# Query projection as block products of 256 columns, second-sweep weights from DRAM, phi turned through DRAM

## The chip, the cores and the metric

The kernel runs on one core of a Trainium2 chip. The metric is the time of one execution on the device, in microseconds (us), the median of several runs. A profile is one further execution, taken by the hardware profiler. The engines are TensorE (PE; its weight loads are shown as PEld), VectorE (DVE), ScalarE (ACT), GpSimd (POOL) and SyncE (SP), which issues nearly all DMAs from one queue that works in order.

## The reference

```python
# x: 2048 x 512; 32 heads of 16
def _A_ref(x, wqkv, w_phi, wo):
    qkv = (x @ wqkv) ...                       # q, k, v per head
    pq = einsum("bhsd,hdf->bhsf", q, w_phi)    # pk likewise
    phi_q = concat([softmax(pq), softmax(-pq)], -1)     # phi_k likewise
    kv = einsum("bhsf,bhsd->bhfd", phi_k, v)
    z  = einsum("bhsf->bhf", phi_k)
    num = einsum("bhqf,bhfd->bhqd", phi_q, kv)
    den = einsum("bhqf,bhf->bhq", phi_q, z)[..., None] + 1e-6
    return (num / den) ... @ wo
def _B_ref(x, w1, b1, w2, b2):                 # 512 -> 1792 -> 512
    h = einsum("bsd,df->bsf", x, w1) + b1
    r = where(h > 0, h, 0)
    return einsum("bsf,fd->bsd", r * r, w2) + b2
g = sigmoid((x * gate_w).sum(-1, keepdims=True))
return g * _A_ref(x, ...) + (1 - g) * _B_ref(x, ...)
```

All data are 32-bit floats.

## The kernel before

Each operand of a large matrix product is split into a rounded high part and the rest, the low part (`split`: ACT writes the high part, DVE or POOL subtracts it). `mm3` makes one product by three matmuls: high by high, high by low, low by high.

The rows are cut into 4 blocks of 512, each with 4 row chunks of 128; two chunks of a block are a pair, so there are 8 pairs. The 1792 hidden columns of the FFN (part B) are cut into 14 of 128. The kernel walks over all blocks twice. Each sweep does half of the FFN, 7 hidden column blocks `fc`, for each row block: 56 steps `t` in all, 28 in each sweep. A step has an `up` (12 matmuls into PSUM pool `ps_u`), ACT's relu, square and rounding, the low part `hl`, and two steps later four `down` (12 matmuls, which gather in four banks over the 7 steps of a block). At the end of a block, DVE adds the gathered rows to a row in SBUF: the first sweep writes it to `part` in DRAM, the second reads it back and writes the output.

Beside the FFN, the first sweep computes k and v of a pair by seven block products of 512 columns (`p1` to `p7`, with sums of the operands: `rows_make` and `rows_ready` for x, `sums_make` and `operand_ready` for the weights), phi of k (`features`), and the sums over rows `kvps` (`do_kv`). `w_phi` is folded into the weights of q and k on the chip (`fold`). The second sweep computes, pair by pair: q by `project` (12 matmuls of 512 columns a chunk); the two exponentials (`exps`: maximum, minimum, two subtractions on DVE, the exponential on ACT); their sums (`sums`); the weighting with z on POOL and the denominator (`q_phi`); and phi turned so that heads lie along partitions (`transposed`: a transpose of 32 x 32 squares on DVE, then four copies on ACT and twelve DMAs a chunk into the tile `phiT`). Then come the numerators (`numer`, 32 small matmuls a pair) and the product with `wo` (`attended`, called by `finish`, 12 matmuls a chunk), which is added to the same row as the FFN's result.

What is done beside step `t` is put in slots: slot `2t` runs before the step's `up`, slot `2t + 1` after it; the second sweep begins at slot 56. `at(slot, f, ...)` fills them. Within this, the order on each engine comes from the framework's scheduler: it goes by the order of the program, `tc.high_priority` moves an instruction ahead, and `tc.issue_after(i)` keeps an instruction behind `i` on the same engine. All waits between engines follow from the tiles.

In the first sweep the weights of a step are fetched again for each block (raw, and rounded again on ACT; the low part from `lkept` in DRAM). In the second sweep all 7 pairs of weight blocks stay in SBUF: three in the pool `fpool`, four in places of operands that the first sweep no longer needs (`ffn_tiles`).

Of the kernel before, what the change touches and what calls it, by code (L numbers as in the profile page):

```python
# [16 lines left out]
P = 128  # L17
# [13 lines left out]
AHEAD = 150  # L31
FOLD_AT = 9, 3
KEPT_LATE = ("w1", 0), ("w1", 1), ("w2", 0)
SUMS = ("t1", "t2", "t15", "k2")
# [3 lines left out]
def tile_gated_mix(ctx: ExitStack, tc: tile.TileContext, xT, xn, wqT, wkT, wphi, wv, wo, w1, b1, w2, b2, gw, out):  # L38
# [16 lines left out]
    taken = [0]  # L55

    def bank(name):
        p = banks[taken[0] % len(banks)]
        taken[0] += 1
        return p.tile([P, 512], F32, tag="s", name=name)  # L60

# [14 lines left out]

    ALL = slice(0, 512)
# [11 lines left out]
    def slots(op, kk, name, dtype=F32R):  # L91
        return [wpool.tile([P, 512], dtype, tag=f"{op}{kk}{j}", name=f"{name}{j}") for j in "hl"]

    def ffn_tiles(nm, fc):
        if fc >= NFH + NSTR:
            return slots(("B21", "T1", "T4", "T3")[fc - NFH - NSTR], int(nm == "w2"), f"{nm}{fc}")
        return (fpool.tile([P, 512], F32R, tag=nm + "h", name=f"{nm}h{fc}"),
                fpool.tile([P, 512], F32R, tag=nm + "l", name=f"{nm}l{fc}"))
# [20 lines left out]

    def again_ready(nm, fc):  # L120
# [15 lines left out]
    def x_tiles(b, k):  # L136
        return (xpool.tile([P, SB], F32R, tag="xh", name=f"xh{b}_{k}"),
                xpool.tile([P, SB], F32R, tag="xl", name=f"xl{b}_{k}"))


    def x_save(b):
        for k in range(NK):
            for j in range(2):
                nc.sync.dma_start(xkept[b, k, j], st["x", b][k][j].bitcast(F32))

    def load_x(b):
        xs = []
        for k in range(NK):
            xs.append(x_tiles(b, k))
            for j in range(2):  # L150
                nc.sync.dma_start(xs[k][j].bitcast(F32), xkept[b, k, j])
        return xs
# [31 lines left out]
    xkept = dram.tile([NB, NK, 2, P, SB], F32, name="xkept")  # L184
    lkept = dram.tile([NFH, 2, P, 512], F32, name="lkept")
    kvs = const.tile([P, 2 * P], F32, name="kvs")
# [53 lines left out]
    def foldq_fetch():  # L240
        st["wq"] = [row() for _ in range(NK)]
        for k in range(NK):
            nc.sync.dma_start(st["wq"][k], wqm[k])

    def foldq_ready(k):
        hi, lo = slots(("B11", "T2")[k // 2], k % 2, f"wq{k}")
        with tc.high_priority(offset=AHEAD):
            split(st["wq"][k], hi, lo, nc.scalar, nc.vector)
        st.setdefault("wa", []).append((hi, lo))
# [9 lines left out]
    def operand_ready(op, kk):  # L259
# [5 lines left out]
        st["W", op, kk] = hi, lo  # L265


    def rows_make(p):
        b, q = divmod(p, 2)
        a, c = (t.rearrange("p (k c s) -> p k c s", k=2, c=NC) for t in st["xr", b])  # L270
        part_of = lambda t, h: t[:, :, 2 * q + h, :]
        r = st["S", p] = [row(), row()]
        o = [r[i // 2][:, i % 2 * 2 * P:(i % 2 + 1) * 2 * P].rearrange("p (k s) -> p k s", k=2) for i in range(4)]
        for i, x, y, op in ((0, part_of(a, 1), part_of(c, 1), ALU.add), (1, o[0], part_of(a, 0), ALU.subtract),
                            (2, part_of(a, 0), part_of(a, 1), ALU.subtract), (3, part_of(c, 0), o[1], ALU.subtract)):
            nc.gpsimd.tensor_tensor(o[i], x, y, op)  # L276

    def rows_ready(p):
        if p % 2 == 0:
            his, los = ([work.tile([P, 512], F32R, tag=g, name=f"S{p}{g}{j}", bufs=2) for j in range(2)] for g in ("oh", "ol"))  # L280
        else:
            t = work.tile([P, 2, 4, NG, 32], F32R, tag="phiT", name=f"S{p}", bufs=1).rearrange("p u r g s -> p (u r g s)")
            t = [t[:, i * 512:(i + 1) * 512] for i in range(4)]
            his, los = t[:2], t[2:]
        for src, hi, lo in zip(st.pop(("S", p)), his, los):
            with tc.issue_after(st["act"].ins):
                split(src, hi, lo, nc.scalar, nc.vector)
        for i in range(4):
            for kk in range(2):
                s = slice((i % 2 * 2 + kk) * P, (i % 2 * 2 + kk + 1) * P)  # L290
                st["A", p, f"S{i + 1}", kk] = his[i // 2][:, s], los[i // 2][:, s]

# [7 lines left out]
    def load_w(src):  # L300
        res = []
        for k in range(NK):
            t = stage.tile([P, 512], F32, tag="in", name="in")
            for q in range(4):
                s = 64 * (4 * (k % 2) + q) + 32 * (k // 2)
                nc.sync.dma_start(t[32 * q:32 * q + 32, :], src[s:s + 32, :])
            if k < 2:
                hi, lo = slots("B22", k, f"wo{k}")
            else:
                hi, lo = (wpool.tile([P, 512], F32R, tag=tag, name=f"wo{tag}") for tag in SUMS[2 * k - 4:2 * k - 2])  # L310
            split(t, hi, lo, nc.scalar, nc.vector)
            res.append((hi, lo))
        return res
# [24 lines left out]
    def project(c, xs, ws, nm):  # L338
        ps = bank(nm)
        sc = slice(c * P, (c + 1) * P)  # L340
        for k in range(NK):
            mm3(ps, xs[k], ws[k], sc, ALL, k == 0, k == NK - 1)
        return ps

    def exps(ps, tag="e"):
# [6 lines left out]
        with tc.high_priority(offset=AHEAD):  # L352
            nc.vector.tensor_reduce(mx, pv, AX.X, ALU.max)
            nc.vector.tensor_reduce(mn, pv, AX.X, ALU.min)
# [517 lines left out]
```

## Time and profile before

| | |
|---|---|
| time, median of 3 runs | 508.5 us (507.81 to 508.73) |
| profiled execution | 506.81 us, its span on the core 505.0 us |
| PE busy | 500.7 us (99%), 3616 matmuls |
| PE weight loads | 404.0 us (80%) |
| DVE busy | 405.2 us (80%) |
| ACT busy | 253.9 us (50%) |
| POOL busy | 75.6 us (15%) |
| DMA | 84.79 MB, mean 168 GB/s |

Busy times are those of one engine; the engines work beside one another, so they do not add up. Matmuls follow each other before the earlier one has left the array, so the length of a row of PE is not its price; the distance between starts is. In a group's row stand the line, the engine, the operation, what it writes and reads, how often, and then the busy time in us, the mean in ns, and the idle time of the engine just before, with what ended it. In a row of the order of time stand the start and the length in us. A row of a stretch has its length and the busy time of each engine, with the number of instructions, then the granted clock of TensorE, the share of the DMA engines and GB/s.

### The profile page before, as it was taken

What the parts mean: (1) busy time and instruction counts of PE and PEld (TensorE: products, weight loads), DVE (VectorE), ACT (ScalarE), POOL (GpSimd) and SP (SyncE); (2) the same over time, 40 slices, a digit from 0 to 9 for tenths busy, and PEclk for the clock granted to TensorE, in tenths of its full rate; (3) what the DMA queues carried; (4) which work ended last, traced back from release to release, by engine and by line L of the source; (5) the groups of instructions that cost most, each with busy time, mean ns of one, the idle gap of its engine ahead of it and who ended that gap; (6) DMA issues with size and microseconds to landing.
All of it is one profiled execution on the core that took longest, in us unless ns stands there. A gap on an engine that the chain in (4) does not pass through costs nothing.

```text
span 505.0 us, 9519 instructions
## 1 busy us (share of the span) xinstructions
PE 500.7 (99%) x3616; PEld 404.0 (80%) x3616; DVE 405.2 (80%) x642; ACT 253.9 (50%) x433; POOL 75.6 (15%) x77
## 2 busy tenths in 40 slices
PE   9999999999999999999999999999999999999997
PEld 4878887788888888888888878787887878788876
DVE  4979996898877868797889898968789677798724
ACT  6598573364743646373765653443425353433530
POOL 5304020302050000000004122202122222202100
PEclk9999999999999999999999999999999999999999
DMA  8998888965657656845669161212153321032102
GB/s 296 331 361 299 232 283 270 321 234 192 212 183 245 236 165 208 279 140 155 187 183 311 51 195 52 91 51 92 39 185 96 86 74 44 8 100 82 43 22 83
DMA packets 52437, 84.79 MB, mean 168 GB/s; under 512 B 8104, under 2 KB 14504, under 8 KB 52392
## 3 DMA queue, kind: packets, MB, share of 16 engines
q1 hardware_dynamic: 52072, 83.79, 51.5%
q8 instruction: 28, 0.46, 0.4%
q10 hardware_dynamic: 288, 0.39, 0.3%
q14 instruction: 17, 0.14, 0.1%
q0 software_dynamic: 32, 0.01, 0.0%
HBM read 56.37 MB, written 21.50 MB: 154 GB/s over the span
## 4 chain that ended last, share of the span: by engine, by line
PE 97%; ACT 1%; DMA 1%; DVE 0%; issue 0%
PE d L75 10%; PE u L75 10%; PE d L77 10%; PE d L76 10%; PE u L76 10%; PE u L77 10%; PE q L75 3%; PE q L77 3%; PE att L77 3%; PE q L76 3%; PE att L76 3%; PE att L75 3%; PE ky L75 2%; PE ky L76 2%; PE ky L77 2%; PE kvps L378 2%
## 5 line engine op out<-in xcount | busy, mean ns | idle before, releaser
L459 ACT ACTIVATE r<-u,b1c 128x512 f32<-128x512 f32 x56 | 38.4, 685 | 146.1 <-PE u L77 146.0
L387 POOL TENSOR_TENSOR ez<-e,z 128x512 f32<-128x512 f32 x32 | 41.3, 1312 | 279.8 <-ACT e L358 160.5
L75 PE MATMUL d<-w2h,hh 128*128 128x512 f32 x160 | 62.7, 392 | 0.0
L77 PE MATMUL d<-w2h,hl 128*128 128x512 f32 x160 | 62.3, 389 | 0.0
L76 PE MATMUL d<-w2l,hh 128*128 128x512 f32 x160 | 62.3, 389 | 0.0
L75 PE MATMUL u<-xh,w1h 128*128 128x512 f32 x152 | 59.6, 392 | 0.1
L76 PE MATMUL u<-xl,w1h 128*128 128x512 f32 x152 | 59.2, 389 | 0.0
L77 PE MATMUL u<-xh,w1l 128*128 128x512 f32 x152 | 59.2, 389 | 0.0
L363 DVE TENSOR_REDUCE sm<-e 128x64 f32<-128x1024 f32 x32 | 38.9, 1215 | 18.5 <-ACT e L358 18.5
L464 DVE TENSOR_TENSOR hl<-r,hh 128x512 fp32r<-128x512 f32 x56 | 38.5, 687 | 13.8 <-ACT hh L463 13.7
L411 ACT ACTIVATE phiT<-tb 32x256 f32<-32x256 f32 x64 | 26.5, 413 | 32.1 <-DVE tb L405 31.4
L358 ACT ACTIVATE e<-e 128x1024 f32<-128x1024 f32 x32 | 33.8, 1056 | 11.9 <-DVE e L356 11.6
L463 ACT ACTIVATE hh<-r 128x512 fp32r<-128x512 f32 x56 | 35.3, 630 | 1.5
L460 ACT ACTIVATE r<-r 128x512 f32<-128x512 f32 x56 | 35.2, 629 | 1.3
L75 PEld LDWEIGHTS d<-w2h,hh 128*128 128x128 f32 x160 | 30.0, 188 | 6.7 <-issue 0.6
L77 PEld LDWEIGHTS d<-w2h,hl 128*128 128x128 f32 x160 | 30.0, 188 | 6.3
L76 PEld LDWEIGHTS d<-w2l,hh 128*128 128x128 f32 x160 | 30.1, 188 | 6.1
L75 PEld LDWEIGHTS u<-xh,w1h 128*128 128x128 f32 x152 | 28.5, 188 | 7.6 <-issue 0.8
L276 POOL TENSOR_TENSOR row<-xin 128x256 f32<-128x256 f32 x16 | 17.5, 1103 | 112.8 <-DVE S2ol L70 24.8
L77 PEld LDWEIGHTS u<-xh,w1l 128*128 128x128 f32 x152 | 28.5, 188 | 6.1
L76 PEld LDWEIGHTS u<-xl,w1h 128*128 128x128 f32 x152 | 28.5, 188 | 5.8
L389 DVE TENSOR_REDUCE dz<-ez 128x64 f32<-128x1024 f32 x16 | 19.4, 1210 | 9.4 <-POOL ez L387 9.3
(544 smaller groups left out, 1161.6 us busy)
## 6 DMA issues: line engine op xcount, KB each, us to landing
in<-in_w SPq DMA_DIRECT2D x66, 256.0 KB, 3.3
phiT<-tb SPq DMA_DIRECT2D x192, 32.0 KB, 1.9
w2l<-lkept SPq DMA_DIRECT2D x20, 256.0 KB, 3.7
w1l<-lkept SPq DMA_DIRECT2D x19, 256.0 KB, 4.4
xin<-in_xT SPq DMA_DIRECT2D x16, 256.0 KB, 5.0
xkept<-xh SPq DMA_DIRECT2D x16, 256.0 KB, 3.6
xkept<-xl SPq DMA_DIRECT2D x16, 256.0 KB, 4.0
in<-in_xn SPq DMA_DIRECT2D x16, 256.0 KB, 2.8
```

The lines of the kernel that those rows point to most:

```text
L75: nc.tensor.matmul(o, ah[:, sa], bh[:, sb], start=first, stop=False, **kw)
L76: nc.tensor.matmul(o, ah[:, sa], bl[:, sb], start=False, stop=False, **kw)
L77: return nc.tensor.matmul(o, al[:, sa], bh[:, sb], start=False, stop=last, **kw)
L358: nc.scalar.activation(ef, ef, AF.Exp)
L363: nc.vector.tensor_reduce(sm, e3, AX.X, ALU.add)
L387: nc.gpsimd.tensor_tensor(ez[:, hs, :], e3[:, hs, :], zbc[half], ALU.mult)
L389: nc.vector.tensor_reduce(dz, ez, AX.X, ALU.add)
L411: nc.scalar.activation(dst, src, AF.Copy)
L459: nc.scalar.activation(r, ps, AF.Relu, bias=b1c[:, fc:fc + 1])
L460: nc.scalar.activation(r, r, AF.Square)
L463: st["act"] = nc.scalar.activation(hh, r, AF.Copy)
L464: low = lambda: st.update(low=nc.vector.tensor_tensor(hl, r, hh.bitcast(F32), ALU.subtract))
```

## The change

1. q of a pair comes from seven block products of 256 columns (`q1` to `q7`), with sums of x chunks (fetched again, `rows_fetch`, and summed on POOL, `rows_again`) and of the folded weights (`foldq_sums`, on POOL). `project` goes. Results are put together by two ACT copies and five DVE additions into two rows in SBUF, from which `exps` reads.
2. The second sweep's FFN weights no longer stay. High and low part lie in one tile and are kept in DRAM (`fkept`), and each step rereads 512 KB for w1 and for w2 (`again_both`). Eleven of the fourteen are split in the first sweep (`early`, `early_ready`, `early_keep`, slots 28 to 45), low parts on POOL.
3. phi goes after DVE's transpose to DRAM in one DMA a chunk (`phi_keep`) and returns turned by four DMAs a pair (`phi_load`). The four ACT copies and twelve DMAs a chunk go.
4. From the end of the first sweep on, the order on PE, DVE and POOL is that of the program (`in_turn`, `Turns`); slots have fractions that order the work within one, and work with a fraction over 0.6 of an odd slot runs between the second and third `down`. `q_phi` is cut into `do_z`, `do_d`, `do_m`, `do_t` with slots of their own.
5. Low parts of the hidden rows `hl` go from DVE to POOL for all second-sweep column blocks but the last two, at the end of the step. Low parts of `wo` go to POOL too. `att` and `kvt` use `ps_u`.
6. High and low parts of x lie in one tile too, with one DMA for both.

```diff
-    def project(c, xs, ws, nm):
-        ps = bank(nm)
-        for k in range(NK):
-            mm3(ps, xs[k], ws[k], sc, ALL, k == 0, k == NK - 1)
...
+EARLY = tuple((nm, NFH + i) for i in range(6) for nm in ("w1", "w2"))[:11]
+HW = D // 2
...
+        def __getattr__(self, name):
+            def issue(*a, **kw):
+                with tc.issue_after(st[self.key].ins) if self.key in st else nullcontext():
+                    i = getattr(self.engine, name)(*a, **kw)
+                if "pe" in st:
+                    st[self.key] = i
+                return i
...
+    vec, pol = Turns(nc.vector, "dve"), Turns(nc.gpsimd, "pool")
...
+    def again_both(nm, fc):
+        w = up_w if nm == "w1" else down_w
+        w[fc] = ffn_tiles(nm, fc)
+        nc.sync.dma_start(st["ffn", nm, fc].bitcast(F32), fkept[fc - NFH, int(nm == "w2")])
...
-            for r in range(4):
-                dst = pt[32 * j:32 * j + 32, u, r, :, :].rearrange("p g s -> p (g s)")
-                src = tb[32 * r:32 * r + 32, 256 * j:256 * j + 256]
-                if j == r:
-                    nc.scalar.activation(dst, src, AF.Copy)
-                else:
-                    nc.sync.dma_start(dst, src)
+    def phi_keep(n):
...
+        nc.sync.dma_start(st["pk", n // 2][n % 2], st.pop(("tb", n)))
+
+    def phi_load(pair):
+        pt = st["pt", pair] = work.tile([P, 2, 4, NG, 32], F32, tag="phiT", name="phiT", bufs=1)
         for j in range(4):
+            nc.sync.dma_start(pt[32 * j:32 * j + 32].rearrange("p u r g s -> p (u r) (g s)"),
+                              st["pk", pair].rearrange("u (r p) (j c) -> j p (u r) c", p=32, c=2 * P)[j])
...
-        low = lambda: st.update(low=nc.vector.tensor_tensor(hl, r, hh.bitcast(F32), ALU.subtract))
+        eng = pol if NFH <= fc < NF - 2 else vec
+        low = lambda: st.update(low=eng.tensor_tensor(hl, r, hh.bitcast(F32), ALU.subtract))
...
+    def q1(p):
+        st["X", p] = ps_a.tile([P, 512], F32, tag="s", name="qx")[:, :HW]
+        product(st["X", p], p, "A11", "B11", True, False)
+        t = kept("t1")
+        st["t1", p], st["t2", p] = t[:, :HW], t[:, HW:]
+        with tc.high_priority(offset=AHEAD):
+            nc.scalar.activation(st["t1", p], st["X", p], AF.Copy)
+
+    def q6(p):
+        st["Y", p] = ps_b.tile([P, 512], F32, tag="s", name="qy")[:, :HW]
+        product(st["Y", p], p, "S2", "T2", True, False)
+        total(st["t2", p], st["Y", p], st["t1", p])
+
+    def q2(p):
+        product(st["X", p], p, "A12", "B21", False, True)
+        st["row", p] = [wpool.tile([P, 512], F32, tag=f"B221{j}", name=f"q{j}") for j in "hl"]
+        with tc.high_priority(offset=AHEAD):
+            nc.scalar.activation(st["row", p][0][:, :HW], st["X", p], AF.Copy)
+
+    def q5(p):
+        st["Z", p] = ps_a.tile([P, 512], F32, tag="s", name="qz")[:, :HW]
+        product(st["Z", p], p, "S1", "T1", True, False)
+        st["t15", p] = kept("t2")[:, :HW]
+        total(st["t15", p], st["Z", p], st["t1", p])
+    # q7: Y += S3 T3, row[1] right = Y + t15;  q3: Z += S4 B22, row[0] right = Z + t2
+    # q4: Y += A22 T4, row[1] left = Y + t1
...
+        for nm, s in (("w1", 2 * t - 8), ("w2", 2 * t - 4)):
+            if (nm, fc) in EARLY and t < (NB + 1) * NFH:
+                i = EARLY.index((nm, fc))
+                k = (28, 29, 30, 37, 38, 39, 40, 41, 42, 43, 44)[i]
...
+            if t < (NB + 1) * NFH and (nm, fc) not in EARLY:
+                at(s, fetch, nm, fc)
+                at(s + 2, ready, nm, fc, pol)
+                at(s + 5, keep_both, nm, fc)
+            else:
+                at(s + 1, again_both, nm, fc)
...
     for p in range(NB * NC // 2):
-            at(s + 2 * c, do_q, NB + q, n + c, n % NC + c)
-            at(s + 2 * c + 2 * (p == 0), do_q_scaled, n + c, n % NC + c)
-        at(t - 2, do_n, p)
+        m, n, s = NPAIR + p, 2 * p, 54 + 6 * p
+        at(s - 6, rows_fetch, m)
+        at(s - 5 + 3 * (p == 0), rows_again, m)
+        at(s - 2, rows_ready, m, pol)
+        for f, d in ((q1, 0), (q6, 1.2), (q2, 1.2), (q5, 2.2), (q7, 2.2), (q3, 3), (q4, 3)):
+            at(s + d + (d == 0 and p > 1) + 0.7 * (p == 1 and d == 3), f, m)
+        u = s + 3
...
+                        (do_e, 0, 0), (do_z, 0, 1), (do_e, 1, 1), (do_s, 0, 1), (do_z, 1, 2), (do_s, 1, 2.8), (do_d, 0, 2.8), (do_m, 0, 3),
+                        (do_t, 0, 3), (do_d, 1, 3), (phi_keep, 0, 4), (do_m, 1, 4.5), (do_t, 1, 4.5), (phi_keep, 1, 5.5)):
...
+        at(u + 6 - 0.5 * late, phi_load, p)
...
+        at(s + 11.7, do_n, p)
+        at(s + 13.1, finish, n, n % NC)
+        at(s + 14.1, finish, n + 1, n % NC + 1)
```

More of the change, by code (lines that the diff above doesn't have):

```diff
@@ new lines, in do_d, with do_m, do_t @@
+        vec.reciprocal(den, den)
+        w = st["w", n] = small.tile([P, H, 2], F32, tag="w", name="w", bufs=2)
+        vec.tensor_tensor(w, r.rearrange("p (h t) -> p h t", t=2),
+                          den.unsqueeze(2).to_broadcast([P, H, 2]), ALU.mult)
+    def do_m(n):
+        st["phi", n] = scaled(st.pop(("q", n))[0], st.pop(("w", n)).rearrange("p h t -> p (h t)"), vec)
+    def do_t(n):
+        tb = st["tb", n] = work.tile([P, 2 * D], F32, tag="tb", name="tb", bufs=2)
+        vec.transpose(tb, st.pop(("phi", n)))
@@ L419, in numer @@
     def numer(pt):
-        pss = [bank(f"num{r}") for r in range(2)]
+        pss = [banks[r].tile([P, 512], F32, tag="s", name=f"num{r}") for r in range(2)]
         def mm(t, q, r):
@@ L481, in up @@
         else:
[L482 to L483 removed]
+            with in_turn():
+                for k in range(NK):
+                    up_step(ps, k, xs, wf)
+            if "pe" in st:
+                st["pe"] = st["up"]
         return hidden(fc, ps, later)
```

355 lines of the change are left out of this document (205 added, 150 removed).

## The prediction

> **What bounds the kernel now.** I read the page first (busy shares, then the chain that ended last), then busy time by stretch, then the groups with their shapes kept apart, the order of time around two places, and the DMA issues.
>
> ```profile
> span 505.0 us, 9519 instructions
> ...
> PE 97%; ACT 1%; DMA 1%; DVE 0%; issue 0%
> ...
> core 0: us, PE busy (x) PEld busy (x) DVE busy (x) ACT busy (x) POOL busy (x), PEclk, DMA share, GB/s
> 0.00:250.50 250.50, 249.31 (x2172) 200.50 (x2176) 205.84 (x332) 143.66 (x240) 34.31 (x45) 1.00 0.74 242
> 250.50:502.00 251.50, 251.35 (x1449) 203.50 (x1448) 198.97 (x311) 110.25 (x193) 41.30 (x32) 1.00 0.31 94
> 280.00:480.00 200.00, 200.00 (x1069) 161.37 (x1068) 163.08 (x250) 88.24 (x157) 36.20 (x28) 1.00 0.27 81
> ...
> 125.00:205.00 80.00, 80.00 (x833) 65.87 (x833) 63.70 (x105) 44.81 (x73) 6.58 (x8) 1.00 0.64 211
> ```
>
> The chain is TensorE's own queue, 97%. In the second sweep (250.5 to 502) TensorE is idle for 0.15 us in 251.5, at a granted clock of 1.00. So there is no wait to take away: that stretch gets shorter only if TensorE gets less to do, and every new wait of TensorE adds its full length. DVE is the second load, 163.08 of 200 us (82%), with POOL at 18% and DMA at 0.27.
>
> **The sum on TensorE.** The kernel projects queries, for each of 16 row chunks, by 12 matmuls of 512 columns (four blocks of the contraction, three products each for the high and low parts): 192. The change makes them pair by pair: seven products, each 2 blocks by 3, so 42 matmuls of 256 columns for a pair, 336 for eight.
>
> ```profile
> 316.10 0.39 PE L75 MATMUL q<-wq0h,xh 128*128 128x512 f32 x1
> ...
> 318.82 0.39 PE L75 MATMUL u<-xh,w1h 128*128 128x512 f32 x1
> ...
> 500.26 0.28 PE L75 MATMUL end<-w212h,hh 128*128 128x256 f32 x1
> ...
> 500.38 0.19 PEld L77 LDWEIGHTS end<-w212h,hl 128*128 128x128 f32 x1
> ...
> 501.57 0.28 PE L77 MATMUL end<-w213h,hl 128*128 128x256 f32 x1
> ```
>
> A duration here contains the pipeline, so the price is the distance of starts. The twelve matmuls of one chunk take 318.82 - 316.10 = 2.72 us, 0.2267 each. The nearest row for the new shape is the last accumulation of the kernel, with new weights for every matmul as in the products: twelve of 256 columns start from 500.26 to 501.57, 1.31 / 11 = 0.119 each. That is a little over half; each pays some 12 ns whatever its width. Removed: 192 x 0.2267 = 43.5 us. Added: 336 x 0.119 = 40.0 us. The gain is 3.5 us, not the eighth (5.4 us) that the count of columns gives. The other matmuls keep their shapes and numbers; the numerators and the attention output move in the order only.
>
> The weight load shows 0.19 us, more than 0.119, yet the loads of these twelve keep the pace: they overlap one another and the matmuls. [...]
>
> **What the other engines gain and lose.** All of it lies beside TensorE; the cover is the time of one pair:
>
> ```profile
> 324.42 1.02 PE num L424 x32
> 352.86 1.02 PE num L424 x32
> ...
> L363 DVE TENSOR_REDUCE sm<-e 128x64 f32<-128x1024 f32 x32 | 38.9, 1215 | 18.5 <-ACT e L358 18.5
> L464 DVE TENSOR_TENSOR hl<-r,hh 128x512 fp32r<-128x512 f32 x56 | 38.5, 687 | 13.8 <-ACT hh L463 13.7
> L405 DVE STREAM_TRANSPOSE tb<-e 128x1024 f32<-128x1024 f32 x16 | 19.9, 1241 | 0.3
> L369 DVE TENSOR_TENSOR e<-e,w 128x1024 f32<-128x1024 f32 x16 | 19.6, 1223 | 0.4
> L389 DVE TENSOR_REDUCE dz<-ez 128x64 f32<-128x1024 f32 x16 | 19.4, 1210 | 9.4 <-POOL ez L387 9.3
> L365 DVE RECIPROCAL r<-sm 128x64 f32<-128x64 f32 x32 | 17.3, 541 | 0.0
> L353 DVE TENSOR_REDUCE mx<-q 128x32 f32<-128x512 f32 x16 | 10.8, 674 | 6.8 <-PE q L77 6.8
> L620 DVE TENSOR_TENSOR kvs<-kvs,kvps 128x256 f32<-128x256 f32 x8 | 3.2, 405 | 0.0
> L387 POOL TENSOR_TENSOR ez<-e,z 128x512 f32<-128x512 f32 x32 | 41.3, 1312 | 279.8 <-ACT e L358 160.5 <-DMA z<-zrow 116.9 <-DVE dz L389 2.4
> L276 POOL TENSOR_TENSOR row<-xin 128x256 f32<-128x256 f32 x16 | 17.5, 1103 | 112.8 <-DVE S2ol L70 24.8 <-DVE T10l L70 24.2 <-DMA xin<-in_xT 22.3
> L411 ACT ACTIVATE phiT<-tb 32x256 f32<-32x256 f32 x64 | 26.5, 413 | 32.1 <-DVE tb L405 31.4
> ```
>
> A pair takes 352.86 - 324.42 = 28.4 us (three up/down steps, two projections, two attention outputs, one set of numerators), 28.0 after. DVE per pair is now 0.82 x 28.4 = 23.2 us. It loses three low parts of the hidden rows (3 x 0.69), which go to POOL, and gains five additions of 256 columns (5 x 0.41, the nearest row is kvs): 23.2 again, 83%. Its low parts of second-sweep weights go to POOL, 11 of 14 in the first sweep. ACT loses the 64 copies into phiT (26.5 us) and gains two copies of 256 columns and two high parts per pair: never near its limit. POOL grows most, per pair: 4 x 1.31 for the z products as now, 3 x 1.31 hidden rows, 2 x 1.31 low parts, 4 x 1.10 row sums = 16.2 us, 58%. A hidden row's low part has more than one whole step before it is read, so I cost these at nothing.
>
> POOL's growth is not quite free for DVE:
>
> ```profile
> 265.23 2.56 POOL L387 TENSOR_TENSOR ez<-e,z 128x512 f32<-128x512 f32 x2 [116.85 <-DMA z<-zrow]
> ...
> 266.75 1.58 DVE L70 TENSOR_TENSOR w111l<-in,w111h 128x512 fp32r<-128x512 f32 x1
> 268.26 0.68 DVE L70 TENSOR_TENSOR w2l<-in,w2h 128x512 fp32r<-128x512 f32 x1
> ...
> 260.00:280.00 20.00, 20.00 (x89) 16.55 (x89) 20.00 (x31) 10.87 (x19) 5.10 (x4) 1.00 0.86 278
> ...
> L394 DVE SCALAR_TENSOR_TENSOR den<-dz,eps x16: 238/252/836, 272.0 to 473.1; 128x32 f32<-128x32 f32 x16
> ```
>
> The same subtraction takes 1.58 us beside POOL's ez and 0.68 just after it ends; den's median is 0.25 and its longest 0.84. [...] From the rows: about twelve such DVE operations a pair (four of them new, since the exponents' subtractions now read q from SBUF and not from PSUM), each meeting POOL with probability 0.58 and waiting half of a 1.31 operation on average, 0.38 x 12 = 4.6 us; some 1.4 of that is there today at 18%. Added 3 us: DVE at about 26 of 28 us. It still fits, with little to spare.
>
> **The new chain from q to the numerators.** phi was turned by 12 small DMAs and four ACT copies a chunk. Now it goes to DRAM in one DMA a chunk, and comes back by four.
>
> ```profile
> phiT<-tb SPq DMA_DIRECT2D x192, 32.0 KB, 1.9
> w2l<-lkept SPq DMA_DIRECT2D x20, 256.0 KB, 3.7
> w1l<-lkept SPq DMA_DIRECT2D x19, 256.0 KB, 4.4
> xin<-in_xT SPq DMA_DIRECT2D x16, 256.0 KB, 5.0
> part<-row SPq DMA_DIRECT2D x16, 256.0 KB, 3.3
> ...
> L67 ACT ACTIVATE xh<-xin 128x512 fp32r<-128x512 f32 x16 | 9.4, 621 | 3.4 <-DMA xin<-in_xT 3.2
> ...
> SPq L413 <- DVE tb L405: 22.6, 9, 7.8
> ```
>
> A keep of 512 KB is not in the trace: between 3.3 (part<-row, half the bytes) and 7, I take 5. The load of 1 MB in four: between 3.7 and 8, I take 6. On DVE, both chunks of a pair: four row operations (2.7), sum and reciprocal (1.75), dz and its four small ones (2.3), scaling and transpose (2.5) = 9.2 each, 18.5 for two, plus the earlier pair's low parts and additions, 3: 21.5, and 32.5 us with the DMAs. TensorE between the last product and these numerators, by the slots of the diff: four ups and four and a half downs (23.1), 42 products (5.0), two attention outputs (5.4), one set of numerators (1.3) = 35 us. Margin 2.5 us; the 3 us of contention or a block's end (four additions of 0.7) use it up. So I charge 0.5 us in all: a fraction of a microsecond at some of the eight pairs, between 0 and 1 us at every one.
>
> SP's queue is in order: a keep waits there for DVE's transpose, as the phiT issues do now (22.6 us in nine waits), and behind it stand the rereads of 512 KB weights. These have three slots and more (some 13 us) before use against a landing of 5; hidden. Rereads (53 x 0.5 MB), phi (16 MB both ways) and x rows (4 MB), less phiT and the raw weights, add some 40 MB in 251 us: 94 + 160 = 254 GB/s, about the 242 that the first sweep moves without a stall. There, eleven early weights add 8 MB in about 80 us: 211 + 103 = 314 GB/s from 125 to 205 us, at a share that 0.64 would put at 0.95; the cover is the two steps between a fetch and its use. I cost it at nothing; the other end is one late landing with its wait, 5 us. ACT, 44.81 of 80 us busy there, takes 11 more high parts of 0.62 us (xh), POOL 11 low parts and earlier row sums, at 6.58 of 80. The rest is small and has that cover too: seven query operands are split for four before, their four sums go to POOL, wo's low parts go from DVE to POOL, and pairs of 256 KB tiles become one of 512 KB with half the issues on SP.
>
> The tail (last accumulation, addition, output) and the start keep their work. Sum: 505.0 - 3.5 + 0.5 = 502.0 us of span. The profiled execution took 506.8 in all, the median of the runs is 508.5; the same 3.0 less gives **505.5 us**.
>
> **Rivals.**
> 1. phi comes late: the numerators of every pair wait about 1 us for its return, because DVE is held up by POOL. 8 x 1.0 - 3.5 = +4.5: 513 us. It decides from 0.44 us a pair. For it: DVE at 26 of 28 us and the margin of 2.5. Against: each wait gives DVE time to catch up, and DVE was at 100% from 260 to 280 with TensorE never waiting. 16%.
> 2. Nothing to measure: waits of 2.5 to 4.5 us at the products (TensorE waits for ACT's copy between the first and third product, or for an addition before it writes on the same bank) use up the gain. 508.5 us. 12%.
> 3. The loads bound the products, at 0.19 us each: 336 x 0.19 - 43.5 = +20 us, 528. The twelve rows of 0.119 speak against it. 3%.
> 4. The first sweep's DMA at 0.95 brings weights late, once or twice by a landing of 5.0 us (xin): 508.5 - 3.0 + 5.0, 510.5 us, or 515.5 for two. 7%.
>
> **How the numbers follow.** The forecast has 62%, alone 504.4 (the full gain and the scatter of runs) to 507.4. A measurement of this kernel tells about 0.2% (1.0 us) from no change. Faster: 62%; same: 12%; slower 16 + 3 + 7 = 26%. The range that leaves out two in ten reaches into rivals 1 and 4: 504.4 to 511.
>
> **What would show it.** Products 0.119 us apart; TensorE's idle time from 250 to the end still under 1 us; numerators 28.0 us apart. Wrong, if weight loads stand 0.19 apart, if the numerators wait for a DMA, if products wait for DVE or ACT, or if DVE's subtractions read 1 us and more beside POOL.

## The result: 6.7% slower

The changed kernel took 542.39 us (median of 6 runs, 538.81 to 548.4), the kernel before on the same chips 507.6 us (6 runs, 506.89 to 508.73): a ratio of 1.0665 [1.0617, 1.0714], where the brackets hold the 95% interval. The longest run, 548.4 us, was in a slower state of the chip, and the ratio leaves it out. The forecast was 505.5 us, range 504.4 to 511. The profiled execution took 539.66 us.

The page of the changed kernel (head, busy shares, and the chain that ended last):

```profile
span 537.9 us, 9771 instructions
...
PE 511.3 (95%) x3760; PEld 413.7 (77%) x3760; DVE 440.2 (82%) x647; ACT 244.7 (45%) x404; POOL 187.5 (35%) x167
...
PE 52%; DVE 23%; DMA 14%; ACT 4%; issue 3%; SPq 2%; POOL 1%; ACTq 0%; DVEq 0%; POOLq 0%
```

The chain was TensorE's own queue for 97%; now it is for 52%, and DVE and DMAs hold 37%. Busy time by stretch, with the columns of the prediction's table:

```profile
0.00:250.50 250.50, 249.00 (x2166) 200.20 (x2167) 205.33 (x326) 147.54 (x246) 59.09 (x65) 1.00 0.81 275
250.50:534.50 284.00, 262.30 (x1596) 213.47 (x1594) 234.38 (x321) 97.14 (x158) 128.42 (x103) 0.98 0.71 229
280.00:480.00 200.00, 183.83 (x1054) 149.58 (x1052) 175.99 (x235) 67.02 (x109) 99.22 (x79) 0.97 0.73 235
```

The first sweep lost nothing to speak of (249.00 us of TensorE, 249.31 before). The second is 284.0 us long instead of 251.5. TensorE is idle for 21.7 us of it, against 0.15, and its mean granted clock is 0.98. No engine is full: DVE 88%, POOL 50%. What TensorE waited for (us in total, times, longest):

```profile
PE num L474 <- DMA phiT<-phi: 11.7, 8, 2.5
PE qy L82 <- DVE t L64: 4.0, 5, 1.3
PE qz L82 <- DVE t L64: 3.4, 2, 3.2
PE qx L82 <- ACT t L683: 1.4, 1, 1.4
```

The numerators wait for phi's return from DRAM, and the products for DVE's additions, which must read a PSUM bank before a product writes it again. The order of time around the longest product wait, on PE, DVE and POOL (start, length; DVE's last line is a quiet `den` from a later pair):

```profile
291.69 0.39 PE L84 MATMUL d<-w,hl 128*128 128x512 f32 x1
295.30 0.58 PE L82 MATMUL qz<-wqB22h,S 128*128 128x256 f32 x1 [3.22 <-DVE t L64]
...
296.32 0.41 PE L83 MATMUL qz<-wqB22l,S 128*128 128x256 f32 x1
296.53 0.41 PE L84 MATMUL qz<-wqB22h,S 128*128 128x256 f32 x1
...
288.10 1.36 DVE L64 SCALAR_TENSOR_TENSOR dz<-dz,inv,r 128x64 f32<-128x64 f32 x1
289.49 1.18 DVE L64 SCALAR_TENSOR_TENSOR den<-dz,eps 128x32 f32<-128x32 f32 x1
...
291.35 2.31 DVE L64 TENSOR_TENSOR e<-e,w 128x1024 f32<-128x1024 f32 x1
293.69 1.25 DVE L64 STREAM_TRANSPOSE tb<-e 128x1024 f32<-128x1024 f32 x1
294.86 0.39 DVE L64 TENSOR_TENSOR t<-qz,t 128x256 f32<-128x256 f32 x1
...
387.52 0.25 DVE L64 SCALAR_TENSOR_TENSOR den<-dz,eps 128x32 f32<-128x32 f32 x1
...
288.08 1.29 POOL L64 TENSOR_TENSOR hl<-r,hh 128x512 fp32r<-128x512 f32 x1
289.33 1.29 POOL L64 TENSOR_TENSOR w<-in,w 128x512 fp32r<-128x512 f32 x1
291.30 1.28 POOL L64 TENSOR_TENSOR w<-in,w 128x512 fp32r<-128x512 f32 x1 [0.68 <-ACT w L74]
```

This one place holds most of the case. Read DVE against POOL: `dz` ends at 289.46, just after POOL's `hl` (289.37); `den` ends at 290.67, just after POOL's `w` (290.62), 1.18 us for work of 0.25; `e<-e,w` takes 2.31 instead of the 1.22 of before. The addition `t` that TensorE needs stands behind this phi work in DVE's written order, and the product starts 3.6 us after the matmul ahead of it (295.30 against 291.69), where 0.23 us is the pace. Then read the products: 0.21 us apart, not 0.12. The granted clock in two slices of 1 us shows why:

```profile
296.00:297.00 1.00, 1.00 (x7) 1.00 (x7) 0.01 (x1) 0.00 (x0) 0.00 (x0) 0.50 1.01 410
299.00:300.00 1.00, 1.00 (x6) 0.82 (x5) 1.00 (x3) 0.23 (x1) 0.00 (x0) 1.00 0.94 299
```

TensorE ran at half clock from 294.9 to 298.3. Four such stretches of 3.4 us (from 294.9, 308.6, 342.7 and 496.3) come at waits in this sweep or just behind them. There the loss is more than the wait: TensorE was busy for 12.9 us of the four stretches, and half of that, about 6.5 us, is my estimate of the price of the clock.

The other wait, in the chain that ended last:

```profile
390.81 1.26 DVE tb L64
...
392.09 2.91 DMA phi<-tb
...
396.37 8.07 DMA phiT<-phi
...
404.57 1.09 PE num L474 x30
```

From the end of the pair's last transpose to its numerators there are 12.5 us: the keep 2.9, 1.4 in SP's queue, the loads 8.1. (Two of the 32 matmuls of the numerators had started at 402.08; the other 30 waited.)

The account, from the distance of each matmul's start to the one before it, less the pace of its shape: numerators about 15.5 us late in all, `qy` 4.8, `qz` 3.9, `qx` 1.5, `kvps` about 2, together 27.7; half clock 6.5; less 3.3 from the products. That is about 31 of the sweep's 32.5; the rest is many small ones.

### The profile page after: what moved, and what is told of

The parts are those of the page before. It is cut to its first block, busy times and chain, and to the rows that moved or that the text cites. A ratio compares the mean times of both kernels' runs of the same rounds, so it can differ in the third digit from the quotient of the medians.

```text
span 537.9 us, 9771 instructions
## 1 busy us (share of the span) xinstructions
PE 511.3 (95%) x3760; PEld 413.7 (77%) x3760; DVE 440.2 (82%) x647; ACT 244.7 (45%) x404; POOL 187.5 (35%) x167
## 4 chain that ended last, share of the span: by engine, by line
PE 52%; DVE 23%; DMA 14%; ACT 4%; issue 3%; SPq 2%; POOL 1%; ACTq 0%; DVEq 0%; POOLq 0%
DMA phiT<-phi 8%; DVE e L64 6%; PE d L82 5%; PE d L84 5%; PE d L83 5%; PE u L82 5%; PE u L84 5%; PE u L83 5%; DMA phi<-tb 3%; DVE dz L64 3%; DVE tb L64 2%; DVE den L64 2%; PE ky L82 2%; PE ky L83 2%; PE ky L84 2%
## 5 line engine op out<-in xcount | busy, mean ns | idle before, releaser
L82 PE MATMUL d<-w,hh 128*128 128x512 f32 x222 | 89.4, 402 | 0.0
L83 PE MATMUL d<-w,hh 128*128 128x512 f32 x222 | 87.8, 396 | 0.0
L84 PE MATMUL d<-w,hl 128*128 128x512 f32 x222 | 87.5, 394 | 0.0
L82 PE MATMUL u<-x,w 128*128 128x512 f32 x216 | 84.9, 393 | 0.7 <-issue 0.6
L83 PE MATMUL u<-x,w 128*128 128x512 f32 x216 | 84.4, 391 | 0.0
L84 PE MATMUL u<-x,w 128*128 128x512 f32 x216 | 84.1, 390 | 0.0
L64 POOL TENSOR_TENSOR ez<-e,z 128x512 f32<-128x512 f32 x32 | 46.7, 1477 | 74.3 <-ACT e L405 36.6
L82 PEld LDWEIGHTS d<-w,hh 128*128 128x128 f32 x222 | 42.5, 192 | 12.4 <-issue 3.9
L84 PEld LDWEIGHTS d<-w,hl 128*128 128x128 f32 x222 | 42.4, 191 | 9.2
L83 PEld LDWEIGHTS d<-w,hh 128*128 128x128 f32 x222 | 42.6, 192 | 7.8
L82 PEld LDWEIGHTS u<-x,w 128*128 128x128 f32 x216 | 40.9, 189 | 9.8 <-issue 1.0
L84 PEld LDWEIGHTS u<-x,w 128*128 128x128 f32 x216 | 40.7, 188 | 8.7
L83 PEld LDWEIGHTS u<-x,w 128*128 128x128 f32 x216 | 40.9, 189 | 8.2
L64 POOL TENSOR_TENSOR hl<-r,hh 128x512 fp32r<-128x512 f32 x20 | 26.8, 1339 | 46.7 <-ACT hh L515 46.7
L77 POOL TENSOR_TENSOR early<-early 128x512 fp32r<-128x512 f32 x11 | 14.6, 1324 | 67.4 <-ACT early L74 54.6
L64 DVE TENSOR_TENSOR hl<-r,hh 128x512 fp32r<-128x512 f32 x36 | 29.4, 817 | 7.9 <-ACT hh L515 7.8
```

The costliest lines, as they stand in the source:

```text
L64: i = getattr(self.engine, name)(*a, **kw)
L77: st["low"] = elo.tensor_tensor(lo, src, hi.bitcast(F32), ALU.subtract)
L82: nc.tensor.matmul(o, ah[:, sa], bh[:, sb], start=first, stop=False, **kw)
L83: nc.tensor.matmul(o, ah[:, sa], bl[:, sb], start=False, stop=False, **kw)
L84: return nc.tensor.matmul(o, al[:, sa], bh[:, sb], start=False, stop=last, **kw)
```

## The experiments

Two causes stood against each other: phi's return trip through DRAM, and POOL's new reads of SBUF, beside which DVE's operations last longer (`den` 1.18 us for 0.25 above). The expectations call the first theory A, the second theory B or the port; "port" is a name here, and no run shows where in the chip DVE is held. A third was the written order on DVE. The first runs take one of them away each; the later ones take two away, measure POOL's reads by themselves, look for a remedy, and put the parts into the schedule of before. Ratios are to the kernel before on the same chip, medians in us. Where DVE's "stretch" is given, it is summed over its instructions after 250 us: what each exceeds the lower quartile of its own shape. Before it is 2.2 us, changed 37.1; these sums move by about 1 us with the way shapes are told apart.

**Part 3 undone: phi turned by ACT copies and small DMAs again.**

```diff
 def phi_keep(n):
+    for j in range(4):
+        for r in range(4):       # j == r: ACT copy; else:
+            nc.sync.dma_start(dst, part_of)
-    nc.sync.dma_start(st["pk", n // 2][n % 2], ...)
```

> The changed kernel with part 3 undone: phi goes to phiT by four ACT copies and twelve 32 KB DMAs a chunk again, at the same slots as the keeps. Theory A (the numerators wait because phi's way through DRAM, a 2.9 us keep and some 9 us of loads, is too long for the schedule): the numerators' waits (15.5 us of late starts in the changed kernel) and the half-clock stretches behind them go, span 515 to 520 us of 537.9. [...]

548.13, 1.0785 [1.0744, 1.0826]: no gain at all. TensorE's waits:

```profile
PE num L479 <- DMA phiT<-tb: 6.9, 5, 2.9
PE u L82 <- DMA w<-fkept: 6.4, 4, 3.4
```

In the kernel before, the 24 small DMAs of two chunks held SP's queue for 15.1 us (299.88 to 314.98), some 7.5 a chunk. Here the rereads of weights stand behind them and land late (`u` waits 6.4 us for them): a second wait, in place of part of the first. In the kernel before the weights stayed in SBUF, and no reread stood behind.

**phi loaded from the pair before**, so that the load need not wait for its own keep.

```diff
-  st["pk", pair]
+  st["pk", max(pair - 1, 0)]
```

> The changed kernel, but the loads of phiT read the tile that the pair before has kept (its results are of the wrong pair), so that numerators wait for no keep of their own pair; the loads, their bytes and their slots stay. Theory A: the numerators' late starts fall from 15.5 us to under 3, the products' stay near 10 us, span 517 to 522. Theory B: TensorE, no longer slowed at the numerators, outruns DVE and waits as much more at the products (for additions on the same bank): span 528 to 536.

539.72, 1.0623 [1.0582, 1.0664], no gain, but the experiment missed its aim: the load was still issued on SP behind its own pair's keep, which waits there for the transpose. TensorE's waits at the numerators fell from 11.7 to 7.3 us, and those at `qy` rose from 4.0 to 7.1. The run says nothing against the return trip as a cause.

**POOL's new work left out**: the low parts `hl`, and the sums of x for all pairs but the first. The fetches of x for these sums and ACT's high parts of them fall away too.

```diff
+  if NFH <= fc < NF - 2: return hh, hh
-  at(s - 6, rows_fetch, m); at(..., rows_again, m); at(s - 2, rows_ready, m, pol)
+  if p == 0: ...   # the same three
```

> The changed kernel with POOL's new work left out: the hidden rows' low parts of the second sweep but the last two blocks (the high part stands in their place in the products) and the sums of x and their splits for pairs 1 to 7 (pair 0's are used again, their DMAs go too). POOL falls from 16 to 5 us a pair. Theory B (the port): DVE's scaling falls back from 1.66 to 1.22 us, den from 0.82 to 0.25, the exponents' subtractions from up to 1.5 to 0.68; some 4 us a pair on DVE; late starts fall from 28 us to under 8, span 508 to 514. Theory A: DVE gets faster but phi's trip still makes the numerators late by more than 1 us a pair: span 522 to 530.

529.06, 1.0428 [1.037, 1.0485].

```profile
PE num L474 <- DMA phiT<-phi: 9.5, 6, 2.1
PE num L474 <- DVE e L64: 2.2, 1, 2.2
...
PE qy L82 <- DVE t L64: 0.6, 1, 0.6
```

The product waits are all but gone, the numerators' stay. DVE's stretch falls from 37.1 to 19.4 us.

**The written order on DVE and POOL given up** (left to the scheduler).

```diff
-  vec, pol = Turns(nc.vector, "dve"), Turns(nc.gpsimd, "pool")
+  vec, pol = nc.vector, nc.gpsimd
```

> The changed kernel without the written-out order on DVE and POOL (TensorE's order stays): the scheduler orders them again. Theory C (DVE's queue waits at its head, 20.6 us for ACT's high parts of the numerators among them, while later work is ready): waits at the products and the numerators shrink, span 520 to 528. Theories A and B: the order is not what is late, span within 5 us of 537.9, or longer.

575.1, 1.1333 [1.1296, 1.1371]. The wait moves to `qx`, whose bank is freed only by the numerators' low parts:

```profile
PE qx L82 <- DVE oo L77: 33.0, 6, 10.4
```

So the written order is better than the scheduler's. Whether a third order would be better still, this run does not tell.

**No return trip**: loads read rows kept long before, issued ahead of the keeps.

```diff
-  st["pk", pair]  ...  at(u + 6 - 0.5 * late, phi_load, p)
+  xkept[0, 0:2]   ...  at(u + 3, phi_load, p)
```

> The changed kernel with phi's return made independent of phi: the four loads of a pair read a block of the kept x (so the numerators are of x and not of phi) and stand six slots after the products start, ahead of the keeps in SP's queue; keeps, loads and bytes stay. Theory D (a loop: numerators of pair p, then DVE's low parts of them, which stand in its fixed order ahead of the next pair's sums, scaling and transposes, then keep, load and the next numerators: 33 us a turn against 28 us of TensorE): the loop is cut, DVE's idle time before the numerators' low parts (20.6 us) falls under 6, late starts at the numerators from 15.5 to under 2 and at the products from 10 to under 5, span 508 to 515. Theory B (DVE's own load is too much): the waits move to the products, span 525 to 533.

532.43, 1.0502 [1.0481, 1.0522].

```profile
PE qy L82 <- DVE t L64: 12.2, 7, 3.4
PE qz L82 <- DVE t L64: 2.0, 3, 1.4
```

No wait at the numerators, but the products now wait for DVE for 14.2 us where it was 7.4.

**Both taken away.**

> The kernel of y1 with POOL's new work left out as in x3 too (hidden rows' low parts of the second sweep but the last two blocks, x sums and splits of pairs 1 to 7). If late phi and the port together are all of the loss, TensorE's late starts in the second sweep fall under 4 us, no half-clock stretch is left before the end, and the gain on the products shows: span 501 to 506. If something else slows the second sweep (DMA, TensorE's written order), it stays above 510.

512.61, 1.0101 [1.0081, 1.0122]. By the ratios, POOL's work alone took 2.4% off the time and the return trip alone 1.6%, some 12 and 8 us; the two together took 5.6%, some 29 us, which is more than the sum. The waits above fit this: with one of them gone, TensorE comes to the other sooner. The stretch from 280 to 480:

```profile
280.00:480.00 200.00, 198.41 (x1192) 164.97 (x1191) 180.54 (x267) 68.98 (x110) 47.15 (x33) 1.00 0.79 250
```

Numerators and products in order of time:

```profile
327.36 1.09 PE L474 MATMUL num<-phiT,kvb 64*32 64x256 f32 x32
...
332.59 0.28 PE L82 MATMUL qx<-wqB11h,x 128*128 128x256 f32 x1
...
333.19 0.28 PE L84 MATMUL qx<-wqB11h,x 128*128 128x256 f32 x1
...
355.49 1.09 PE L474 MATMUL num<-phiT,kvb 64*32 64x256 f32 x32
```

First to sixth matmul of a product: 0.60 / 5 = 0.120 us. These two sets of numerators stand 28.13 us apart, forecast 28.0. So the products do what they were to do, and the clock is back at 1.00.

**The numerators' low parts later on DVE**, behind the next pair's `sm` and `dz`, as a test of the idea that DVE's waits in its order feed the loop.

```diff
-  split(pss[r], oh, ol, nc.scalar, vec)
+  nc.scalar.activation(oh, pss[r], AF.Copy)
+  at(s + 11.9, do_nl)      # the low parts
```

> The changed kernel with one edit: DVE's low parts of the numerators stand in its order behind the next pair's sums and denominators (second chunk's sums, first chunk's denominators), not ahead of them. Theory D: DVE no longer waits for the numerators with 4.6 us of work ready, the loop gets some 3 to 4 us shorter, span 518 to 528. Theory A (a long trip alone): the chain from products to numerators is no shorter, span 535 to 541.

553.01, 1.0912 [1.0887, 1.0937]. The idea fell: the low parts also free banks, and `qx` waits for them.

```profile
PE qx L82 <- DVE oo L64: 12.9, 5, 6.1
```

**phi written turned, four keeps of 128 KB, and one plain load a chunk.**

```diff
+  for j in range(4): nc.sync.dma_start(t[j].rearrange("p r c -> r p c"), tb[:, 256*j:256*(j+1)])
+  nc.sync.dma_start(st["pt", n // 2][:, n % 2]..., st["pk", n]...)   # 512 KB, contiguous
```

> The changed kernel with phi laid out in DRAM as phiT needs it: four keeps of 128 KB a chunk, then one contiguous load of 512 KB a chunk, the first chunk's a slot earlier than before. Theories A and D: the trip from the last transpose to the numerators falls from 12.4 to some 8 us, 4 us a pair: late starts at the numerators under 5 us, span 518 to 527. Theory B: DVE is late by itself, waits move to the products, span 530 to 538.

586.41, 1.1546 [1.1499, 1.1593]. From the chain of the last pair, in order of time:

```profile
487.29 7.47 DMA phi<-tb
494.83 3.88 DMA phiT<-phi
```

The waits of SP's queue:

```profile
SPq L467 <- DMA phi<-tb: 80.4, 24, 5.9
```

A load of one chunk took 3.9 us, where a pair, twice the bytes, took 8.1. The keep grew from 2.9 to 7.5 us, and a load that waits on SP for its keep holds up all that stands behind it, 80.4 us in all.

**`wo` loaded later, on top of "both taken away"**, for the wait of `kvps` (2.6 us) that was left there.

```diff
-  at(base + 10 + k, load_w, wo, k)
+  at(57 + k, load_w, wo, k)
```

> The kernel of y2 (phiT loaded from kept x, POOL's hidden-row low parts and x sums left out) with one more edit: wo is loaded and split in slots 57 to 60, not 52 to 55, so that ACT's queue does not wait for it at the turn of the sweeps. In y2 TensorE waits 2.8 us there before the last sums over rows. Theory E (what y2 still loses is the turn of the sweeps): that wait goes, span 505 to 508. If it stays, another head of ACT's or POOL's queue holds it: 509 to 512.

513.25, 1.0119 [1.0076, 1.0161]: the wait fell to 1.0 us, the time did not.

**Split sums of x kept in DRAM**, not computed again on POOL, so that the change is complete but POOL lighter.

```diff
+  at(split_at + 4, rows_save, p)     # 1 MB a pair to DRAM
-  at(s - 6, rows_fetch, m); at(..., rows_again, m); at(s - 2, rows_ready, m, pol)
+  at(s - 2, rows_load, m)
```

> The changed kernel, results whole, with the split sums of x kept in DRAM in the first sweep and read back (1 MB a pair) where the change fetches x again and forms and splits its sums on POOL. POOL loses 5.6 of 16 us a pair. Theory F (late phi and the port each hide the other): DVE's stretching falls by a quarter to a third, but the numerators still wait for the trip, so the span falls by 2 to 7 us only, 531 to 536. Theory B alone (the port is all): 520 to 527.

543.37, 1.0709 [1.0688, 1.0729]. POOL falls from 99 to 62 us in 280 to 480, but with 8 MB of keeps more, at 305 GB/s, TensorE is busy for 3.7 us less of the first sweep (249.00 in the changed kernel):

```profile
0.00:250.50 250.50, 245.35 (x2139) 196.13 (x2140) 202.04 (x322) 146.29 (x245) 55.81 (x61) 0.99 0.87 305
```

**That, `wo` late, and each chunk's loads issued on their own as early as may be.**

> The kernel of z2, results whole, with wo in slots 57 to 60, and with the first chunk's loads of phi issued ahead of the second chunk's landing, so that 512 KB and not 1 MB stand behind the last keep. Theory F: both hold-ups shrink together, the trip by some 3 us and the port by a third, which is worth more than each alone: span 512 to 524, still not under 505. Theory B or A alone would give 525 to 533.

544.73, 1.0712 [1.0667, 1.0758]. The numerators still wait 9.7 us, `qy` 6.4. No complete version was found that gives the time back.

**Is it POOL's reads, or POOL's time?** On "both taken away", POOL writes a scratch tile for as long as the left-out work took.

```diff
+  for _ in range(n): pol.memset(scratch, 0.0)     # n = 4, 11, 8
```

> The kernel of y2 (phiT from kept x; hidden rows' low parts and x sums left out), with memsets of POOL in the places of what was left out, 4 of 128x256 (0.32 us each) for a hidden row's low part, 11 for a pair's sums and 8 for their low parts, into a tile that nobody reads: POOL is as busy as in the changed kernel, but these operations read nothing. Port theory (DVE's operations with two SBUF inputs wait for POOL operations that read SBUF): the product waits stay away, DVE's stretching stays near y2's 16 us, span 509 to 514. POOL-late theory (DVE waits for the z products, which stand behind other work in POOL's order): product waits come back, span 522 to 530.

513.63, 1.0101 [1.006, 1.0142], as without. POOL's group of writes:

```profile
L64 POOL MEMSET scratch<- 128x256 f32 x213 | 66.4, 312 | 11.3
```

The stretch from 280 to 480:

```profile
280.00:480.00 200.00, 198.90 (x1197) 165.43 (x1196) 180.86 (x268) 70.31 (x113) 104.12 (x216) 1.00 0.79 249
```

POOL is as busy as in the changed kernel (104 us; 99 there) and TensorE loses nothing. DVE's stretch is 16.5 us, against 16.0 with POOL light and 33.4 with POOL's real work. So a busy POOL is not what cost the time: its reads of SBUF held up DVE. One group of DVE without the return trip, first with POOL's real work:

```profile
L64 DVE TENSOR_TENSOR e<-e,w 128x1024 f32<-128x1024 f32 x16 | 26.3, 1641 | 0.2
```

and with POOL light:

```profile
L64 DVE TENSOR_TENSOR e<-e,w 128x1024 f32<-128x1024 f32 x16 | 19.5, 1219 | 0.2
```

With the memsets this group's mean is 1411 ns, and that of `den` 538 where it is 708 with POOL light: the sums of the stretch agree, its places do not.

Which operations of DVE are held shows in the changed kernel, after 250 us, in the mean over the rows that a row of POOL lies beside and over those that stand alone. With two inputs in SBUF they are longer: `den` 1.17 us against 0.25, `w` 0.86 against 0.22, `e<-e,w` 2.01 against 1.21, `e<-qh,mx` 1.02 against 0.68. With one input they are not: `sm` 1.20 and 1.21, the transpose `tb` 1.25 and 1.25, the reciprocal of `den` 0.35 and 0.35. Nor are they with one of two in PSUM: `ql<-qy,t` 0.42 (3 rows) and 0.43, `row<-d,rest,row` 0.74 (12 rows) and 0.74.

POOL's new work is not the only reading that meets DVE. Of the 16 us of stretch that stay with POOL light, some 12 are those of `den` and `w` (708 and 544 ns in the mean of 16 each, 252 and 225 in the median of the kernel before). In the changed kernel eight of 16 `den` lie beside `ez`, the product with z, which POOL computed in the kernel before too. There one of 16 did, and DVE's whole stretch is 2.2 us: the small operations of a chunk mostly came when `ez` was over. The new order (part 4) puts the `ez` of one chunk beside the `den` and `w` of the other. In the changed kernel:

```profile
379.49 1.17 DVE L64 SCALAR_TENSOR_TENSOR den<-dz,eps 128x32 f32<-128x32 f32 x1
...
379.28 2.58 POOL L64 TENSOR_TENSOR ez<-e,z 128x512 f32<-128x512 f32 x2 [4.10 <-ACT r L512]
```

With POOL light, the group of `den`:

```profile
L64 DVE SCALAR_TENSOR_TENSOR den<-dz,eps 128x32 f32<-128x32 f32 x16 | 11.3, 708 | 0.6
```

What this part of the order costs in time, no run here shows.

**Each half of POOL's work alone**, on "no return trip".

> The kernel of y1 with the hidden rows' low parts (3 x 1.34 us a pair on POOL) alone left out; the x sums stay. By POOL's time the sums and their low parts are the larger half (some 6 us a pair): if the harm goes by POOL's reading time, 40 % of the 20 us between y1 and y2 come back: span 520 to 525.

> The kernel of y1 with the x sums and their splits of pairs 1 to 7 alone left out; the hidden rows' low parts stay on POOL. By POOL's reading time 60 % of the 20 us come back: span 515 to 520. If one of the two sets everything (the sums stand right beside the products' additions), this one alone reaches 512 and v2 stays at 528.

Without `hl` 522.51, 1.0289 [1.0262, 1.0316]; without the sums 520.73, 1.0282 [1.0225, 1.0339]. From 532.43 to 512.61 there are 20 us, and each half is about 10: the cost grows with the work. The half without `hl` changes POOL's work alone; without the sums their fetches and ACT's high parts fall away as well, so that half is not POOL's alone.

**`hl` back on DVE, all else as changed** (`eng = vec`).

> The changed kernel, results whole, with the hidden rows' low parts on DVE in all blocks, as before the change, at the end of the step. DVE gains 3 x 0.6 us of its own a pair and loses three meetings with POOL of some 0.35 us each: about even, span 533 to 545. If moving them to POOL was the main harm, under 528.

544.91, 1.072 [1.0687, 1.0754]: about even with 542.39, as expected. That DVE spends on `hl` what it no longer loses beside POOL was the reason given before the run; the run shows the even result and not the reason.

**The parts in the schedule of before.** phi through DRAM, without the rest:

```diff
+  at(s + 2 * c + 2 * (p == 0) + 2, phi_keep, n + c)
+  at(t - 5, phi_load, p)
```

> The kernel before with part 3 alone: phi goes to DRAM in one keep a chunk and returns by four loads a pair, five slots ahead of the finish, three ahead of the numerators; nothing else is changed. Theory G (the trip is harmful only where both chunks of a pair start their exponents after the last product and the numerators stand 8.7 slots on): here the first chunk starts two slots earlier, the numerators lie six slots behind the last transpose; span 503 to 507. If a trip through DRAM costs by itself: over 510.

`hl` on POOL, without the rest:

```diff
+  eng = nc.gpsimd if NFH <= fc < NF - 2 else nc.vector
```

> The kernel before with the hidden rows' low parts of the second sweep (all blocks but the last two) on POOL, nothing else changed. DVE loses 20 x 0.6 us and meets POOL some 20 times more, at up to 1 us; TensorE had no wait there and DVE some 50 us of idle time in the sweep. Slack theory (the port hurts only where TensorE has a wait on DVE): span 504 to 507. Port theory without slack: over 510.

And both:

> w1 and w2 together on the kernel before: phi through DRAM, and the hidden rows' low parts on POOL. If the costs only add there: w1's 5.8 us plus w2's. If they hide and then multiply as in the changed schedule, at least 5 us more than the sum.

In this order: 513.09, 1.0112 [1.0083, 1.0141]; 508.03, 1.0007 [0.9988, 1.0025]; 515.18, 1.0151 [1.0128, 1.0173]. The return trip alone costs 1.1% even there, with one wait of TensorE of 2.6 us. `hl` on POOL costs nothing measurable: DVE has slack (busy for 159.90 of 200 us), and TensorE is busy throughout (`hl` on POOL alone, 280 to 480):

```profile
280.00:480.00 200.00, 200.00 (x1067) 160.98 (x1066) 159.90 (x239) 89.67 (x160) 57.49 (x44) 1.00 0.28 83
```

With both, TensorE has one long wait:

```profile
PE att L75 <- DVE ol L70: 3.9, 1, 3.9
```

And the stretch of 20 us around it is partly at half clock:

```profile
300.00:320.00 20.00, 16.12 (x86) 12.44 (x86) 12.68 (x19) 5.08 (x9) 4.20 (x3) 0.83 0.67 197
```

The half clock lasts from 306.1 to 312.9, and TensorE was busy for 4.95 us of it. 3.9 us of wait and half of 4.95 us are 6.4 of the 8.8 us that the span grew by (513.8 against 505.0). No kernel here was faster than the one before.

## Why the prediction was wrong

- **The sum on TensorE held.** 336 matmuls at 0.120 are 40.3 us; 0.119 was taken. The gain is 43.5 - 40.3 = 3.2 us, 3.5 forecast. Rival 3 (weight loads at 0.19 bound the products) is excluded by the rows at 0.120.
- **The first sweep held.** 249.00 us of TensorE, and 79.42 of 80 us from 125 to 205. DMA moved 269 GB/s there, forecast 314. Rival 4 did not occur.
- **The failed step is the chain from q to the numerators, "I charge 0.5 us in all".** It put 32.5 us against 35 of TensorE's work, a margin of 2.5. At the pair whose return was shown, DVE's last addition for q starts at 364.89 and the numerators at 404.57: 39.7 us. By terms: DVE 27.2 (to 392.07) where 21.5 was put, the keep 2.9 for 5, SP's issues 1.4 for none, the loads 8.1 for 6. The largest miss is DVE: in its rows there, six operations are longer beside POOL than quiet ones by 4.1 us together, and DVE stands 1.8 us waiting for ACT's copy of the numerators before. The 3 us of contention had been set against DVE's total and named as something that would use up the margin, at a price of 0.5 us; on a chain it is a term of the sum, and with it alone the margin was negative. No run shows the 0.38 us a meeting from which those 3 us were formed, which was an estimate; the runs show 37.1 us of stretch on DVE after 250 us where 2.2 were before, 4.4 us more a pair. Less the 4.1 us the chain would still be 35.6 us, and with POOL light the numerators did wait as long as before (9.5 and 2.2 us).
- **The total of DVE was close and misled.** Forecast was "about 26 of 28 us" a pair. Between 340.34 and 492.70, five pairs, DVE is busy for 136.4 us, 27.3 a pair; its share is 90% only because a pair lasts 30.5 us. A share below one does not say that each result is in time: DVE's rows keep their written order, and the addition that frees a bank stands behind stretched phi work (`t` at 294.86, behind the 6.8 us of DVE's rows from 288.10 on).
- **The argument against rival 1 failed.** "Each wait gives DVE time to catch up" does not hold where DVE waits for TensorE in turn:

```profile
L64 DVE TENSOR_TENSOR oo<-num,oo 128x512 fp32r<-128x512 f32 x16 | 10.3, 684 | 20.6 <-ACT oo L74 20.6
```

  In the changed kernel DVE is idle for 20.6 us before the numerators' low parts, which stand in its order ahead of the next pair's sums. Whether another order would help is not settled; the two tried made it worse.
- **Rivals 1 and 2 were priced as alternatives, 513 and 508.5 us.** Both occurred, and the second not for ACT's copy but for DVE's additions, which rival 2 names too. The price of 1 us a pair for phi was too small: 15.5 / 8 = 1.9. And there was no term for the clock, by the estimate above about 6.5 us.
- **POOL and DMA.** POOL was forecast at 16.2 us a pair and shows 14.1 over the same five pairs. DMA was forecast at 254 GB/s in the second sweep and shows 229, but the sweep is longer: the bytes are the same within 2%. As totals both were sized well; what decided was the effect of POOL's reads on DVE, and the return trip.
- **Open.** With both waits gone the kernel still takes 512.61 us, 7 more than forecast. 250.5 to 280 holds 3.1 us of TensorE's idle time, at the turn of the sweeps; the one remedy tried there gained nothing.

## What to carry to other kernels

Where one engine is the bound and idle for 0.15 us in 251, an exchange of work on the others is priced by chains, not by shares: write the chain from each operand to its use with contention and queue gaps as terms, and count a margin of 2.5 us on a chain of 32 as none. Before work moves to GpSimd, count the VectorE instructions with two SBUF inputs that it will run beside, the small ones too: here `den`, 0.25 us alone, took 1.17 us in the mean of the ten that met a GpSimd operation of 1.3 us, and each ended within 0.05 us of that operation's end. A new order can bring about such meetings with work that GpSimd did all along (eight `den` beside `ez`, one before). Two waits in one loop can hide each other (here 12 and 8 us alone, 29 together), so take away both before either is called harmless.

## What the runs showed of the hardware

- Half clock came with short waits, and the length of the wait alone did not decide. In the changed kernel it lasted 3.41 us each time: from 294.92, at the end of a wait of 3.2 us (to 295.30); from 308.58, at the end of one of 2.0 us that followed one of 2.5 us (to 308.93 and 306.32); from 342.71, after waits of 1.2 and 1.0 us (340.34 and 341.89); and from 496.31, after one of 1.97 us (495.28). The wait of 1.88 us that ended at 404.57 had none: the granted clock is 1.00 from 399 to 412. In the kernel of before with both parts it lasted for 6.8 us (306.1 to 312.9) and began 2 us into a wait of 3.9 us. In the changed kernel the later three begin 13.7, 47.8 and 201.4 us after the first, near 4, 14 and 59 times the 3.41 us that each lasted. Why it came where it did, no run here shows.
- A keep to DRAM was slower in pieces: 512 KB from 128 partitions in whole rows took 2.9 us; of four DMAs of 128 KB that scatter pieces of 1 KB, the last landed 7.5 us after its issue, with rereads of weights issued beside it. The way back shows no such difference: 8.1 us for the 1 MB of a pair in four loads into 32 partitions each, 3.9 us for a plain load of the 512 KB of one chunk.
